# Gated linear attention and a rational gelu-like layer on one core: a new order of all steps and loads

## The chip, the cores and the metric

The kernel runs on one core of one Trainium2 chip. The metric is the time of one execution on the device in microseconds (us), as the median over runs. Engines are named as in the profile: PE is TensorE's matmul, PEld its weight load, DVE is VectorE, ACT is ScalarE, POOL is GpSimd, SP is SyncE.

## The reference

Two layers follow each other. The first is a linear attention with a gate per channel, for 4 batches and 8 heads, 768 tokens, 48 channels per head; the second works on its result as 3072 tokens by 384.

```python
f = 1 / (1 + exp(-f_logit))
for t in range(768):                                   # state: [B, H, 48, 48], from zero
    state = f[:, :, t, :, None] * state + einsum('bhd,bhe->bhde', k[:, :, t], v[:, :, t])
    y[:, :, t] = einsum('bhd,bhde->bhe', q[:, :, t], state)

x = y.transpose(0, 2, 1, 3).reshape(3072, 384)
h = x @ w_in                                           # 384 -> 2048
P = a[0] + a[1] * h + a[2] * h**2 + a[3] * h**3
Q = 1 + abs(b[0]) * abs(h) + abs(b[1]) * h**2
out = (P / (Q + 1e-6)) @ w_out                         # 2048 -> 384
```

## The kernel before

**Units.** The work is cut into 12 units of 256 tokens. Unit n is batch n % 4 and chunk n // 4, so four units in a row don't depend on each other, and unit n needs the state that unit n - 4 left. Each unit passes through all steps.

**The order is written out by hand.** A text named `ORDER` lists all steps, separated by semicolons, and the kernel's last loop calls the function of each in turn. Every engine and queue gets its instructions in that order and works them off in that order; between engines only the data dependences hold (semaphores are set by them). So a step that waits holds back everything behind it on its own engine or queue and nothing else. `sc 5 1 @1` means step sc of unit 5 with argument 1 in PSUM slot 1 (there are four, `@0` to `@3`). Arguments such as `8 16` are blocks of 128 of the 2048 columns of h, so `0 16` is a whole step and `8 16` a half; for f, k, q and the steps on them `2 4` is the second half of the heads.

**Attention steps.** `ld n f`, `ld n k`, `ld n q` load 384 KB each from SP's queue, `ld n v` loads from POOL's queue and converts to bf16. `ef`, `ls` (ACT) give log(1 + exp(-f)); `cs` (PE) sums it along the tokens; `A` and `ae` (ACT) are exponentials of that; `xa n 1` and `xa n 0` (DVE, or POOL where a `p` ends the step) multiply k and q by them; `T` (PE) transposes and `Te` (DVE, or ACT with `s`) copies the result from PSUM; `sc` (PE) gives scores, `mk` (DVE) masks them; `vm` (POOL) copies pieces of v; `yi` and `yb` (PE) make y; `ic`, `si` (PE) and `st` (DVE) carry the state on; `ye` (ACT with `s`, DVE with `v`) copies y to x.

**Layer steps.** `h` (PE) multiplies x by w_in, four blocks at a time; `hy` (ACT) copies it to SBUF. `sq` and `ab` (DVE) make h squared and its absolute value, scaled so that Q needs only their sum. That sum is made in one of three ways, half by half: `zv` adds on DVE, `zd` issues from POOL a DMA that accumulates in SBUF, `u` (PE) adds by two matmuls with the identity into PSUM. `lz` (or `ln`, after `u`) takes the logarithm and `ex` the exponential with scale -1, both on ACT: 1 / Q. For P, `p1` (DVE) makes a3 h + a2, `pm` multiplies by h squared, `p2` makes a1 h + a0, and the two are added by `tv` on DVE or by `ta`, again an accumulating DMA from POOL. `gm` (DVE) multiplies P by 1 / Q; `o` (PE) multiplies by w_out; `oe` copies the result from PSUM and `so` stores it from SP's queue, in two DMAs.

```python
def zv(n, m0, m1):
    return nc.vector.tensor_add(fl(big(s, "z"), m0, m1), fl(big(s, "z"), m0, m1), fl(big(s, "h2"), m0, m1))
def zd(n, m0, m1):
    return nc.gpsimd.dma_start(out=fl(big(s, "z"), m0, m1), in_=fl(big(s, "h2"), m0, m1), accum_op=ALU.add)
```

**Buffers.** f, k, q and v have three buffers each, hy and g three, the squares and z two. `ld 7 k` thus waits until `xa 4 1` has read its buffer, and `so` holds back the loads behind it on SP until `oe` is done. **Weights.** `wi 0 8`, `wi 8 16` (three DMAs each) bring w_in, four `wo` bring w_out, all converted to bf16, from POOL's queue. Constants come from `cz`, `cu`, `ci`, `cm`; `ab_`, `fa`, `fb`, `fr` load and prepare the coefficients.

Lines in the profile: L206 load, L214 w_in, L221 w_out, L284 `ef`, L317 `xa`, L360 `mk`, L457 `h`, L469 `hy`, L473 `sq`, L477 `ab`, L485 `u`, L495 `zv`, L499 `zd`, L503 `lz`, L508 `ex`, L513 `p1`, L518 `p2`, L523 `pm`, L527 `ta`, L531 `tv`, L535 `gm`, L544 `o`, L550 `oe`, L559 `so`.

Of the kernel before, what the change touches and what calls it, by code (L numbers as in the profile page):

```python
# [29 lines left out]
h 1 12 16 @2; hy 1 4 8; p1 0 0 16; ls 3; h 1 0 4 @3; lz 0 0 8; ab 0 8 16; cs 2 @1; pm 0 0 16; h 1 8 12 @0  # L30
hy 1 12 16; A 2 1; u 0 12 16 @2; p2 0 0 16; hy 1 0 4; xa 2 1; ae 2; A 2 0; u 0 8 12 @3; ln 0 12 16; tv 0 0 8
hy 1 8 12; xa 2 0; ef 4; ab 1 8 16; T 2 @1; ln 0 8 12; ab 1 0 8; cs 3 @2; sq 1 0 16; Te 2 s; si 2 0 @0; A 3 1
sc 2 0 @3; tv 0 8 16; sc 2 1 @1; ic 2; zd 1 0 8; A 3 0; ae 3; mk 2 0; ex 0 0 16; xa 3 1 0 4 p; u 1 8 12 @2
st 2 0; yb 2 0 2 @3; mk 2 1; vm 3 1; yi 2 1; si 2 1; xa 3 0; u 1 12 16 @1; ls 4; st 2 1; ld 6 q; yb 2 2 4
gm 0 0 8; ld 5 f; ln 1 12 16; cs 4 @0; ld 4 k; ln 1 8 12; gm 0 8 16; ld 6 f; T 3 @1; ld 6 k; ae 4; ye 2 s
p1 1 0 16; o 0 1 8 12 @2; ex 1 8 16; si 3 0 @3; o 0 0 8 12; pm 1 0 16; o 0 1 12 16; o 0 1 4 8; lz 1 0 8
o 0 0 12 16; o 0 0 4 8; p2 1 0 16; ef 5; o 0 1 0 4; Te 3; o 0 0 0 4; A 4 0; ta 1 8 16; A 4 1; ic 3; tv 1 0 8
sc 3 1 @1; ls 5; h 2 12 16 @0; oe 0 0 2 s; mk 3 1; xa 4 1 0 4 p; ld 8 f; ld 7 f; ef 6; sc 3 0 @2; ld 5 q; st 3 0
h 2 8 12 @1; ex 1 0 8; so 0 0 2; mk 3 0; vm 3 0; vm 4 1; si 3 1; xa 4 0; h 2 4 8 @2; hy 2 12 16; gm 1 8 16
# [10 lines left out]
hy 4 0 4; xa 7 0; ic 6 @3; hy 4 8 12; sc 5 0 @1; vm 5 1; ta 3 8 16; o 2 0 8 12 @2; mk 5 0; ef 9; o 2 0 12 16  # L50
vm 6 0; lz 3 8 16; vm 6 1; si 6 0; sq 4 0 16; o 2 1 4 8; yb 5 2 4 @0; yb 5 0 2; lz 3 0 8; yi 5 1; yi 5 0
ab 4 0 16; o 2 0 0 4; T 6 @1; ye 5 s; p1 4 0 16; zd 4 8 16; ls 8; o 2 0 4 8; ld 7 v; st 6 0; h 5 12 16 @0
ex 3 0 16; Te 6; zd 4 0 8; o 2 1 12 16; p2 4 0 16; si 6 1; o 2 1 0 4; h 5 0 4 @1; pm 4 0 16; hy 5 12 16
o 2 1 8 12; hy 5 0 4; h 5 8 12 @0; gm 3 0 8; oe 2 0 2 s; ta 4 8 16; h 5 4 8 @1; gm 3 8 16; hy 5 8 12; lz 4 8 16
# [557 lines left out]
```

## Time and profile before

| | |
|---|---|
| Time, median of 3 runs | 245.29 us (244.83 to 245.74) |
| The profiled execution: its own time, its span | 245.4 us, 243.7 us |
| Granted clock of TensorE, mean | 0.972 |
| Busy: PE, DVE, ACT, POOL | 201.7, 204.6, 196.2, 93.7 us |
| DMA packets of POOL's queue (q0) and of SP's (q1) | 24.92 MB and 18.88 MB |

The profile is of one execution. Busy time is the time in which an engine works on an instruction; DMAs are shown by their queue, packet by packet. "Idle before" tells which event ended an engine's wait. The 1.7 us between the profiled execution's time and its span lie before the first and after the last instruction of the program.

### The profile page before, as it was taken

What the parts mean: (1) busy time and instruction counts of PE and PEld (TensorE: products, weight loads), DVE (VectorE), ACT (ScalarE), POOL (GpSimd) and SP (SyncE); (2) the same over time, 40 slices, a digit from 0 to 9 for tenths busy, and PEclk for the clock granted to TensorE, in tenths of its full rate; (3) what the DMA queues carried; (4) which work ended last, traced back from release to release, by engine and by line L of the source; (5) the groups of instructions that cost most, each with busy time, mean ns of one, the idle gap of its engine ahead of it and who ended that gap; (6) DMA issues with size and microseconds to landing.
All of it is one profiled execution on the core that took longest, in us unless ns stands there. A gap on an engine that the chain in (4) does not pass through costs nothing.

```text
span 243.7 us, 7028 instructions
## 1 busy us (share of the span) xinstructions
PE 201.7 (83%) x3116; PEld 143.9 (59%) x3120; DVE 204.6 (84%) x194; ACT 196.2 (81%) x188; POOL 93.7 (38%) x105
## 2 busy tenths in 40 slices
PE   0468599669999969989829899999999799998792
PEld 0346378436677647767616757787676576854361
DVE  3266299999989999999665799999999999995950
ACT  3354059999999997979609999999999799968950
POOL 6084034040415495374053633654545323441000
PEclk9999889988999999999997999999999999999799
DMA  7999999998999985999959799999999858999352
GB/s 133 228 206 159 122 204 205 198 208 191 223 248 250 180 167 58 192 223 213 202 125 159 121 253 215 206 156 227 211 248 210 168 118 161 185 203 205 86 127 66
DMA packets 64382, 44.24 MB, mean 182 GB/s; under 512 B 53728, under 2 KB 58848, under 8 KB 64352
## 3 DMA queue, kind: packets, MB, share of 16 engines
q0 software_dynamic: 23088, 24.92, 62.8%
q1 hardware_dynamic: 40976, 18.88, 35.3%
q8 instruction: 24, 0.39, 0.7%
q10 hardware_dynamic: 288, 0.00, 0.1%
q14 instruction: 6, 0.05, 0.1%
HBM read 25.17 MB, written 4.72 MB: 123 GB/s over the span
## 4 chain that ended last, share of the span: by engine, by line
DMA 28%; DVE 18%; issue 18%; ACT 17%; PE 7%; POOL 6%; SPq 3%; POOLq 0%; ACTq 0%; DVEq 0%
DMA f<-in_f_logit_dram 9%; DMA g<-hy 6%; DMA w_in_sb<-in_moe_w_in_dram 5%; PE op L544 5%; DVE g L535 5%; ACT qi L508 4%; ACT hy L469 4%; ACT lq L503 4%; DMA v<-in_v_dram 4%; DMA z<-h 4%; SPq L206 3%; DVE h L473 3%; DVE g L513 2%; DVE hy L518 2%; DVE z L477 2%
## 5 line engine op out<-in xcount | busy, mean ns | idle before, releaser
L544 PE MATMUL op<-w_out_sb,g 128*128 128x384 bf16 x384 | 72.8, 337 | 4.1 <-DVE g L535 4.1
L457 PE MATMUL hp<-x,w_in_sb 128*128 128x256 bf16 x576 | 69.6, 275 | 6.2 <-DMA w_in_sb<-in_moe_w_in_dram 2.8
L457 PEld LDWEIGHTS <-w_in_sb 128*128 128x128 bf16 x576 | 56.2, 98 | 17.4 <-issue 5.6
L544 PEld LDWEIGHTS <-g 128*128 128x128 bf16 x384 | 36.9, 101 | 31.0 <-issue 5.5
L469 ACT CAST hy<-hp 128x1024 bf16<-128x1024 f32 x48 | 47.0, 1052 | 9.5 <-PE hp L457 9.5
L508 ACT ACTIVATE qi<-lq 128x2048 bf16<-128x2048 f32 (+1 forms) x19 | 45.1, 2374 | 2.3 <-DVE g L535 2.2
L503 ACT ACTIVATE lq<-z 128x2048 f32<-128x2048 bf16 x21 | 40.5, 1928 | 5.5 <-DMA z<-h 5.5
L499 POOL DMA_DIRECT2D z<-h x19 | 20.4, 1191 | 47.1 <-DVE z L477 31.9
L535 DVE TENSOR_TENSOR g<-g,qi 128x2048 bf16<-128x2048 bf16 (+1 forms) x19 | 30.5, 1627 | 6.9 <-ACT qi L508 5.9
L360 DVE TENSOR_TENSOR scm<-sc,mask 128x1024 bf16<-128x1024 f32 x24 | 28.7, 1215 | 7.5 <-PE sc L352 7.3
L527 POOL DMA_DIRECT2D g<-hy x18 | 19.1, 1109 | 38.2 <-DVE hy L518 17.5
L317 POOL TENSOR_TENSOR qkp<-k,A 128x768 bf16<-128x768 f32 x10 | 24.8, 2479 | 18.2 <-DMA k<-in_k_dram 9.1
L473 DVE TENSOR_TENSOR h<-hy 128x2048 bf16<-128x2048 bf16 (+1 forms) x16 | 28.0, 1751 | 0.2 <-ACT hy L469 0.2
L523 DVE TENSOR_TENSOR g<-g,h 128x4096 bf16<-128x4096 bf16 (+1 forms) x15 | 27.8, 1856 | 0.1
L284 ACT ACTIVATE f<-f 128x768 f32<-128x768 f32 (+1 forms) x13 | 10.8, 833 | 13.6 <-DMA f<-in_f_logit_dram 13.6
L331 PE MATMUL tp<-ident,qkp 128*128 128x128 bf16 x192 | 15.0, 237 | 7.9 <-POOL qkp L317 4.3
L312 ACT ACTIVATE A<-cs 128x768 f32<-128x768 f32 (+1 forms) x26 | 19.8, 800 | 0.7 <-PE cs L304 0.6
L367 POOL COPY vmp<-v 128x128 bf16<-128x128 bf16 x24 | 15.7, 802 | 10.8 <-DMA v<-in_v_dram 8.7
L206 POOL DMA_DIRECT2D v<-in_v_dram x12 | 14.1, 1179 | 12.1 <-PE y L373 11.3
L331 PEld LDWEIGHTS <-qkp 128*128 128x128 bf16 x192 | 12.9, 106 | 9.9 <-POOL qkp L317 4.7
L299 PE MATMUL cs<-lsp,Ui 128*128 128x384 bf16 (+1 forms) x39 | 11.1, 343 | 9.1 <-ACT lsp L289 8.8
L513 DVE TENSOR_SCALAR g<-hy,a_sb 128x4096 bf16<-128x4096 bf16 x12 | 17.7, 1471 | 1.0 <-ACT hy L469 1.0
...
## 6 DMA issues: line engine op xcount, KB each, us to landing
...
```

The lines of the kernel that those rows point to most:

```text
L317: i = (nc.gpsimd if eng == "p" else nc.vector).tensor_mul(s["qk"][:, x, :, hh, 0:D], s["qk"[x]][:, hh].rearrange("p h i d -> p i h d"), s[ ...
L331: nc.tensor.transpose(t[:, x, i, p, :], s["qk"][:, x, i, 2 * p:2 * p + 2, :].rearrange("t h d -> t (h d)"), ident)
L360: return nc.vector.tensor_mul(t, s["sc", g].rearrange("s r a i t -> s (r a) (i t)"), mb)
L457: nc.tensor.matmul(t[:, m - m0, :].rearrange("f (j t) -> f j t", j=UB), w_in_sb[:, kk, m * P:(m + 1) * P], s["x"][:, :, kk, :], start=(kk ...
L469: nc.scalar.copy(fl(big(s, "hy"), m0, m1), fl(s["hp", m0], 0, m1 - m0))
L473: return nc.vector.tensor_mul(fl(big(s, "h2"), m0, m1), fl(big(s, "hy"), m0, m1), fl(big(s, "hy"), m0, m1))
L503: nc.scalar.activation(fl(lq, m0, m1), fl(big(s, "z"), m0, m1), AF.Ln, scale=regs[2], bias=1.0 + 1e-6)
L508: nc.scalar.activation(fl(qi, m0, m1), fl(lq, m0, m1), AF.Exp, scale=-1.0)
L513: return nc.vector.tensor_scalar(fl(big(s, "g"), m0, m1), fl(big(s, "hy"), m0, m1), a_sb[:, 3:4], a_sb[:, 2:3], op0=ALU.mult, op1=ALU.add)
L523: return nc.vector.tensor_mul(fl(big(s, "g"), m0, m1), fl(big(s, "g"), m0, m1), fl(big(s, "h2"), m0, m1))
L535: return nc.vector.tensor_mul(fl(big(s, "g"), m0, m1), fl(big(s, "g"), m0, m1), fl(qi, m0, m1))
L544: nc.tensor.matmul(s["op", g][:, j, 0:DM], big(s, "g")[:, m, C * j:C * j + C], w_out_sb[:, m, :], start=(s["on", j] == 1), stop=(s["on", j ...
```

## The change

Only `ORDER` is replaced: 785 steps become 765. No function changes.

- Every step's place changes, the loads' and stores' on SP and POOL among them. On SP the sequence around unit 7 to 11 was `so 1, ld 8 q, ld 8 k, ld 7 k, ld 10 f, so 3, so 2, ld 9 q, ld 9 k, ld 11 f, ld 11 q, so 4, ld 10 k, ld 10 q, ld 11 k`; it becomes `ld 8 q, ld 7 k, ld 9 f, so 1, ld 8 k, so 2, ld 10 f, ld 11 f, ld 9 k, ld 9 q, ld 10 k, so 3, ld 10 q, so 4, ld 11 q, ld 11 k`.
- The 48 half sums (24 for Q, 24 for P): `zd` 19 to 16, `zv` 2 to 6, `u` 3 to 2 (six quarters to four), `ta` 18 to 19, `tv` 6 to 5. Accumulating DMAs go from 37 to 35, additions on DVE from 8 to 11.
- Halves become whole steps: `ex` 19 instructions to 14, `gm` 19 to 14, `sq` 16 to 13, `ab` 16 to 13, `pm` 15 to 13.
- `xa 1 1` goes from POOL to DVE (10 products on POOL become 9). `Te` on DVE: units 1, 4, 8, 10 and both halves of 0, instead of 1, 3, 6, 7, 10 and those halves; the others on ACT. `ye 6` goes from ACT to DVE. `oe` on DVE: units 7 and the second part of 11, instead of 4, 9 and that part.
- At the start, `cs 2`, `sc 1 0` and `sc 1 1` come ahead of `h 0 0 4`, and `wi 0 8` follows `vm 0 1`, no longer `ld 2 v`. The `wo` loads follow `ta 0 0 8`.

The diff, cut to the start, the places named here and the end:

```diff
@@ -17,80 +17,78 @@
 ORDER = """
-ld 0 k 2 4; cz 1; ld 1 v; ld 0 f 0 2; cz 2; cz 3; cz 0; ld 0 f 2 4; cu 0; ld 0 k 0 2; ld 0 v; ld 0 q 2 4
-ld 0 q 0 2; ci; ld 1 f; cu 1; ld 1 q; ef 0 0 2; ab_ b a; ab_ a a; cm; ld 1 k; ls 0 0 2; ef 0 2 4; cs 0 0 2 @0
-ld 2 f; ls 0 2 4; A 0 1 0 2; cs 0 2 4 @1; vm 1 1; A 0 1 2 4; A 0 0 2 4; xa 0 0 2 4; xa 0 1 2 4; xa 0 1 0 2
-T 0 2 4 @2; Te 0 2 4; ic 0 @3; ef 1; vm 0 1; ld 2 v; sc 0 1 @2; ae 0 2 4; ls 1; mk 0 1; wi 0 8; ae 0 0 2
-A 0 0 0 2; cs 1 @1; xa 0 0 0 2; fa; T 0 0 2 @2; ae 1; A 1 1; si 0 0; vm 0 0; wi 8 16; st 0 0; vm 1 0
-xa 1 1 0 4 p; Te 0 0 2; si 0 1; st 0 1; ef 2; sc 0 0 @0; yi 0 1 @2; mk 0 0; ls 2; ic 1 @3; fr; yb 0 2 4
-yb 0 0 2; A 1 0; si 1 0; ye 0 s; xa 1 0; vm 2 1; ld 4 q; T 1 @0; vm 2 0; ld 3 f; h 0 0 4 @1; ld 2 k; Te 1
-ld 3 k; ld 4 f; sc 1 0 @2; hy 0 0 4; ld 2 q; sc 1 1 @0; ld 3 q; mk 1 1; h 0 4 8 @1; mk 1 0; yb 1 2 4 @0
-hy 0 4 8; st 1 0; yb 1 0 2; fb; yi 1 1; sq 0 0 8; ld 4 v; h 0 12 16 @2; ye 1 s; wo 0 4; ab 0 0 8; h 0 8 12 @1
...
-A 5 1; ic 4 @3; ls 6; ab 2 8 16; yi 3 1; yb 3 2 4; ae 5; sq 2 0 8; ef 7; ld 9 f; zd 2 8 16; T 4 @0; ye 3 s
...
-ye 4 s; zd 3 0 8; oe 1 0 2 s; h 4 12 16 @3; gm 2 0 16; A 7 1; so 1 0 2; A 7 0; ld 8 q; h 4 4 8 @0; ld 8 k
-Te 5 s; pm 3 0 16; h 4 0 4 @2; ld 7 k; ld 10 f; hy 4 4 8; sc 5 1 @1; hy 4 12 16; h 4 8 12 @0; mk 5 1; ta 3 0 8
...
-st 6 1; xa 7 1 0 4 p; sc 6 0 @2; sc 6 1 @0; mk 6 0; o 3 0 4 8 @3; o 3 1 12 16; hy 5 4 8; vm 7 1; mk 6 1
-ta 4 0 8; cs 8 @2; ef 10; p1 5 0 16; yb 6 0 2 @1; A 8 0; yb 6 2 4; ex 4 8 16; yi 6 1; sq 5 0 16; yi 6 0
...
-u 11 12 16 @3; pm 11 0 16; o 9 1 8 12; o 9 1 0 4; o 9 0 4 8; o 9 0 0 4; ln 11 8 12; gm 10 8 16; o 9 0 12 16
-oe 8 0 2 s; gm 10 0 8; o 10 1 12 16 @2; ln 11 12 16; so 8 0 2; o 10 1 8 12; p2 11 0 16; o 10 0 0 4; ex 11 8 16
-o 10 0 8 12; tv 11 8 16; o 10 1 4 8; lz 11 0 8; o 10 1 0 4; gm 11 8 16; o 10 0 12 16; o 10 0 4 8; oe 9 0 2 v
-ex 11 0 8; o 11 1 8 12 @1; tv 11 0 8; so 9 0 2; o 11 0 8 12 @3; o 11 0 12 16; oe 10 0 2 s; gm 11 0 8
-o 11 1 12 16; so 10 0 2; o 11 0 0 4; o 11 0 4 8; o 11 1 4 8; oe 11 0 1 s; o 11 1 0 4; so 11 0 1; oe 11 1 2 v
-so 11 1 2
+ab_ b a; ld 0 f 0 2; cz 1; cu 0; ld 0 f 2 4; cz 3; cz 2; cz 0; ld 0 k 0 2; cu 1; ld 1 f; ld 0 q 2 4; ld 0 v; cm
+ld 0 q 0 2; fa; ci; ef 0 0 2; ld 0 k 2 4; ld 1 v; si 0 0 @0; ef 0 2 4; ld 2 f; ls 0 0 2; ls 0 2 4; cs 0 0 2 @1
+ab_ a a; ld 1 k; cs 0 2 4 @2; ef 1; A 0 0 0 2; A 0 1 0 2; A 0 1 2 4; ae 0 0 2; A 0 0 2 4; ls 1; xa 0 0 2 4
+ld 1 q; xa 0 0 0 2; ae 0 2 4; cs 1 @3; xa 0 1 2 4; xa 0 1 0 2; T 0 2 4 @1; ae 1; A 1 0; ld 2 q; vm 0 1; wi 0 8
+ic 0; A 1 1; Te 0 2 4; T 0 0 2 @2; ef 2; st 0 0; ld 3 f; si 0 1; ls 2; Te 0 0 2; sc 0 1 @1; wi 8 16; st 0 1
+ld 2 k; cs 2 @3; xa 1 1; xa 1 0; sc 0 0 @2; A 2 1; fb; vm 0 0; T 1 @0; A 2 0; mk 0 0; ae 2; fr; mk 0 1
+si 1 0 @3; ic 1; yi 0 1 @2; st 1 0; yb 0 2 4; Te 1; yb 0 0 2; ld 4 f; sc 1 0 @1; ye 0 s; ld 3 v; sc 1 1 @0
+mk 1 0; si 1 1; vm 1 1; vm 1 0; h 0 0 4 @2; mk 1 1; ld 2 v; st 1 1; xa 2 0; h 0 4 8 @1; hy 0 0 4; ld 4 q
+yi 1 1 @0; hy 0 4 8; yb 1 2 4; yb 1 0 2; ab 0 0 8; ef 3; h 0 12 16 @3; sq 0 0 8; ye 1 s; ld 3 q; ls 3
+h 0 8 12 @2; zv 0 0 8; hy 0 12 16; cs 3 @1; xa 2 1; hy 0 8 12; h 1 4 8 @0; lz 0 0 8; ld 6 f; sq 0 8 16
...
+ta 0 0 8; yb 2 0 2; cs 4 @0; wo 12 16; ab 1 0 16; T 3 @2; wo 0 4; ae 4; vm 3 0; st 3 0; ye 2 s; wo 8 12
+p1 1 0 16; si 3 1; A 4 1; h 2 0 4 @1; wo 4 8; Te 3 s; st 3 1; pm 1 0 16; h 2 4 8 @3; A 4 0; sc 3 0 @2; hy 2 4 8
...
+o 0 0 8 12 @3; sq 2 0 16; ln 1 8 12; si 4 0; h 3 4 8 @0; ls 6; lz 1 0 8; T 4 @2; p1 2 0 16; zd 2 0 8; o 0 1 0 4
...
+yi 4 1 @2; yi 4 0; gm 1 0 16; yb 4 0 2; oe 0 0 2 s; yb 4 2 4; so 0 0 2; cs 6 @0; ye 4 s; ld 6 q; h 4 4 8 @1
...
+ld 7 k; sc 5 0 @3; o 1 0 8 12; vm 5 0; st 5 1; xa 6 1 0 4 p; ld 9 f; mk 5 1; o 2 0 0 4 @1; lz 3 0 8; o 2 1 12 16
...
+T 6 @0; so 1 0 2; o 2 0 8 12; ld 8 k; ye 5 s; vm 6 0; st 6 0; zd 4 0 8; p2 4 0 16; ls 7; si 6 1; o 2 1 0 4
+Te 6 s; h 5 12 16 @3; st 6 1; zv 4 8 16; cs 7 @2; oe 2 0 2 s; pm 4 0 16; h 5 0 4 @0; A 7 0; so 2 0 2; ld 10 f
...
+sc 6 0 @1; hy 5 4 8; cs 8 @2; mk 6 1; xa 7 1 0 4 p; lz 4 8 16; o 3 0 12 16 @3; o 3 0 8 12; mk 6 0; ta 4 0 8
...
+pm 5 0 16; h 6 4 8 @0; o 3 0 0 4; o 3 1 0 4; ld 10 k; vm 7 0; st 7 1; hy 6 0 4; xa 8 0; h 6 12 16 @2; ef 10
...
+cs 9 @2; p2 5 0 16; ld 10 q; lz 5 8 16; o 4 1 8 12 @1; mk 7 0; o 4 0 8 12; ta 5 8 16; lz 5 0 8; ab 6 0 16
...
+p1 11 0 16; ln 11 0 4; so 8 0 2; o 9 1 12 16; ln 11 4 8; gm 10 0 8; o 9 0 8 12; ex 10 8 16; o 9 0 12 16
+pm 11 0 8; o 10 1 4 8 @2; o 9 0 4 8; p2 11 0 16; ex 11 0 8; o 10 0 4 8; o 9 1 4 8; gm 10 8 16; o 10 0 0 4
+oe 9 0 2 s; tv 11 0 8; lz 11 8 16; o 10 1 12 16; so 9 0 2; o 10 0 12 16; gm 11 0 8; o 10 1 8 12; ex 11 8 16
+o 10 1 0 4; pm 11 8 16; o 11 1 0 4 @3; o 11 0 0 4 @0; tv 11 8 16; o 11 1 4 8; o 10 0 8 12; gm 11 8 16
+o 11 0 4 8; oe 10 0 2 s; o 11 1 12 16; so 10 0 2; o 11 1 8 12; o 11 0 12 16; oe 11 1 2 v; o 11 0 8 12; so 11 1 2
+oe 11 0 1 s; so 11 0 1
 """
```

More of the change, by code (lines that the diff above doesn't have):

```diff
@@ L30 @@
[L30 to L39, printed above, removed]
@@ L50 @@
[L50 to L54, printed above, removed]
@@ new lines @@
+p1 7 0 16; o 5 0 0 4; hy 8 12 16; ic 9; ab 7 0 16; lz 6 0 8; sc 9 0 @3; sc 9 1 @0; o 5 0 4 8; tv 6 0 8
+o 5 1 8 12; zd 7 0 8; lz 6 8 16; o 5 1 4 8; mk 9 1; xa 10 1 0 4 p; mk 9 0; h 8 4 8 @0; ex 6 0 16; vm 9 1
+zd 7 8 16; xa 10 0; h 8 8 12 @3; vm 9 0; st 9 0; ld 11 v; p2 7 0 16; h 8 0 4 @2; pm 7 0 16; hy 8 8 12
+o 5 1 12 16; o 5 1 0 4; hy 8 4 8; o 5 0 8 12; hy 8 0 4; cs 11 @3; gm 6 0 16; ta 7 8 16; oe 5 0 2 s; ic 10 @0
+ta 7 0 8; A 11 0; yi 9 0 @2; yi 9 1; yb 9 2 4; A 11 1; sq 8 0 16; yb 9 0 2; ae 11; T 10 @1; ye 9 s; lz 7 0 8
```

80 lines of the change are left out of this document (41 added, 39 removed).

## The prediction

> **What bounds the kernel now.** I read the page first (shares and slices), then the sums by stretch, then the timelines of VectorE, ScalarE and SP around the one long gap, and last the DMA queues in short windows. From the page:
>
> ```profile
> span 243.7 us, 7028 instructions
> PE 201.7 (83%) x3116; PEld 143.9 (59%) x3120; DVE 204.6 (84%) x194; ACT 196.2 (81%) x188; POOL 93.7 (38%) x105
> ...
> PE   0468599669999969989829899999999799998792
> ...
> DVE  3266299999989999999665799999999999995950
> ```
>
> Three engines have almost equal work, and VectorE (DVE) has most. Its idle time is 243.7 - 204.6 = 39.1 us. The sums by stretch (length, then busy time by engine) tell where that lies:
>
> ```profile
> 0.00:40.00 40.00, 24.74 (x420) 19.00 (x421) 21.26 (x47) 17.73 (x27) 17.76 (x34) 0.96 1.18 178
> 40.00:120.00 80.00, 70.38 (x1153) 50.58 (x1154) 78.30 (x67) 75.17 (x75) 31.47 (x28) 0.98 1.05 196
> 120.00:140.00 20.00, 13.94 (x206) 10.06 (x206) 12.89 (x10) 13.35 (x13) 9.28 (x8) 0.91 0.80 141
> 140.00:220.00 80.00, 75.69 (x1252) 55.20 (x1252) 79.32 (x62) 74.93 (x67) 34.38 (x35) 1.00 1.01 197
> 220.00:243.70 23.70, 16.90 (x90) 9.07 (x89) 12.84 (x11) 15.06 (x10) 0.82 (x1) 0.93 0.54 119
> ```
>
> The third busy time is VectorE's: idle 18.7 us at the start, 1.7 in 40:120, 7.1 in 120:140, 0.7 in 140:220, 10.9 at the end. So outside start and end VectorE is the bound, with one hole. The timelines of ScalarE and of SP name its cause:
>
> ```profile
> 127.47 0.84 ACT L284 ACTIVATE f<-f 128x768 f32<-128x768 f32 x1 [6.65 <-DMA f<-in_f_logit_dram]
> ...
> 74.36 0.76 SPq L206 DMA_DIRECT2D f<-in_f_logit_dram  x1
> 95.90 1.26 SPq L559 DMA_DIRECT2D out_dram<-osb  x2
> 97.25 1.98 SPq L206 DMA_DIRECT2D q<-in_q_dram  x1
> 99.34 7.25 SPq L206 DMA_DIRECT2D k<-in_k_dram  x2
> 106.64 7.13 SPq L206 DMA_DIRECT2D f<-in_f_logit_dram  x1
> ```
>
> SP stood from 75 to 95.9 us behind the store of unit 1 (`so 1 0 2` waits for `oe 1`). Four loads were then issued together, `ld 7 k` and `ld 10 f` last, and f of unit 10 took 20.8 us to land (median of that load on the page: 6.8 us). Why so long, the DMA queues show in the window 108:112, while accumulating sums move:
>
> ```profile
> q0 software_dynamic: 204, 0.77, 96.6%
> q1 hardware_dynamic: 204, 0.08, 10.1%
> ```
>
> Both queues got 204 packets in 4 us: one each in turn. A sum's packet is 4096 bytes, a load's 384, so POOL's queue took 0.77 MB and SP's 0.08. A load of 384 KB (1024 packets) beside sums needs 1024 / 204 x 4 = 20 us, about what was seen; by q0's rate a sum of 512 KB takes 2.7 us.
>
> **The change, part by part.** The arithmetic of the reference is the same; ORDER is new. Prices are spacings of successive starts in the timeline.
>
> *VectorE's work.* Additions there go from 8 to 11 halves (`zv` 2 to 6, `tv` 6 to 5): 3 x 1.14 (50.83 to 51.97 in the timeline) = +3.4. Halves merged into whole steps: `sq` 3, `gm` net 5, `pm` net 2, each saving 2 x 1.14 - 2.20 = 0.08, and `ab` 3 x 0.08: -1.0. `xa 1 1` moves from POOL to VectorE: +0.9. `Te`: one of full size fewer: -1.1. `ye 6` comes, one `oe` goes: 0.9 - 0.9. Sum **+2.2 us** (1.5 to 3), all of it on the path, since VectorE is the bound.
>
> *POOL's products beside VectorE.* The groups of L513 and L518 last 1.47 and 1.53 us in the mean, 1.33 where undisturbed; one at 81.02 took 3.71 while POOL worked on `xa 5 1`. 24 x 0.17 = 4.1 us for 10 products; 9 remain: **-0.4** (all 4.1 gone, or 4 more).
>
> *The hole.* For each load I added the VectorE work listed between its issue and its first user, and the DMA time of the sums and v loads listed in between (2.7 and 2.3 us each). Before: `ld 7 k` has 15.5 us against 16.0 of DMA time, `ld 10 f` 17.8 against 18.7: just these two were late. After: 17.9 against 7.3 and 16.0 against 8.2. `ld 8 k`, behind `so 1`, has 16.3 against 8.2, `ld 9 f` 19.7 against 12.8. The thinnest of the later loads are `ld 10 q` (24.1 against 23.8) and `ld 11 q` (15.0 against 13.3). Stores still stand between loads on SP, but fewer loads that are soon needed stand behind one. I take 6 of the 7.1 us back, and leave 1.1 for a thin one: **-6.0** (-7.1 to 0).
>
> *Coarser steps.* A whole `gm` now waits for a whole `ex` (3.52 us on ScalarE) in units 1, 6 and 7; for 4, 7 and 8 the list leaves only 3.4 to 3.6 us of VectorE work between the two. Before, one such wait was 3.2 us long, 5.9 in all. **+1.0** (0 to 4).
>
> *The sums.* 35 instead of 37: 2 x 2.7 us less for the DMA engines, -8 matmuls for `u` on PE and two issues of about 1.1 us fewer on POOL. All beside VectorE: 0. If the cover goes (a `lz` that waits for its sum cost ScalarE 5.5 us in all), it is worth up to -2. The list leaves most sums of units 4 to 9 more room than before (`ta 4 0 8` 10.6 us against 8.0, `zd 6 0 8` 13.9 against 8.1).
>
> *w_out.* Its four loads move from behind `ld 4 v` of the start to behind `ta 0 0 8`. Before, the third landed 16.3 us after the first was issued (35.5 to 51.7), and the first `o` began at 59. Now `wo 8 12` is third, and its first user `o 0 0 8 12` stands 14.4 us of VectorE work behind the first issue: 2 us late, of which I take half, as PE then has h of unit 3 behind it but VectorE has a gelu in hand: **+1.0** (0 to 4).
>
> *ScalarE* gets one `Te` more (1.77) and merges (-0.4): +1.4, beside VectorE (9.9 us idle in 40:120 and 140:220 together): 0. If that idle time were gone, +1.4.
>
> *The start.* VectorE begins in earnest at 34.3 (first `sq`). The w_in loads come at 14.0 to 18.5, behind a v load, and gate h: the chain of waits has one of them landing at 28.16, and the upper half lets `h 0 12 16` go only after 33.8. Now `wi 0 8` waits for `vm 0 1`, thus for v of unit 0 alone, and `sc 1 0`, `sc 1 1` stand ahead of `h 0 0 4` on PE, so that masks and products run while w_in lands. VectorE work ahead of the first gelu step grows from 16.0 to 18.2 us: if gelu starts at the same time, **-2.2**. v 0, the first on its queue at about 3.3, with the 7.7 us of the first v load now lands near 11; that would issue w_in 3 us sooner, so -5; the other bound, +10, is the first rival.
>
> *The end.* From the last `gm` on, 16 matmuls and two stores follow, as before; ScalarE has 17.0 us listed behind the last `hy` instead of 16.2, VectorE 18.8 instead of 16.2, where it also waited for 2.6: **0** (-1 to +2).
>
> Sum: 2.2 - 0.4 - 6.0 + 1.0 + 1.0 - 2.2 = -4.4. The profiled execution took 245.4 us (span 243.7), the median of three is 245.3, so it stands for them: 245.4 - 4.4 = **241.0 us**.
>
> The Trainium skill's page "DMA: Bandwidth & Descriptors", section "Queues, rings and completion order", says that a DMA engine drains a whole packet, typically 9 to 17 descriptors, before it turns to the next queue. If a turn carried that many rows of a load, loads would hardly suffer beside sums or w_in, and the first rival would fall away. The 204 against 204 above, at 384 bytes a packet of SP's queue, speak against that.
>
> **Rivals.** *Loads starved by w_in at the start (slower).* In the new order SP still has k and q of unit 1 to bring (ninth and tenth load) when w_in begins. Both stand before `mk 0 0` on VectorE (`xa 1 1`, `xa 1 0`), thus before y, x and h of unit 0. Here 2.7 MB of SP's loads, as many as the new order has up to q of unit 1, landed by 17.9, and only then w_in moved alone. In 26:32, with both, the queues carried:
>
> ```profile
> q1 hardware_dynamic: 982, 0.37, 80.0%
> q0 software_dynamic: 333, 0.37, 49.3%
> ```
>
> That is one load in 6 us. If w_in issued at 11 moves from 13 on and needs the 15.8 us of here (18 to 33.8), it ends at 28.8 and q 1 lands near 30. `xa 1 0`, `fb`, both masks (3.8), then y, x, `sc 1`, two h and two `hy` (7 us by the timeline) bring the first gelu to 40.8: 6.5 later than 34.3, less the 2.2 of work done, +4.3 where the sum has -2.2: 247.5. With w_in slowed to 31.5 and q 1 at 34.3 it is 251.8. I take 249. It decides at one point: whether q 1 has landed when w_in's packets begin. For it speaks the alternation; against it, that `vm 0 1` and `wi 0 8` may come as late as before.
>
> *The hole moves (no change).* `so 2` has `ld 10 f`, `ld 11 f`, `ld 9 k`, `ld 9 q` and `ld 10 k` behind it. If `oe 2` is late by as much as `oe 1` was (SP's 22 us), one is again late: 5 of the 6 us come back, 246.0. Also if the new order does not keep loads and sums apart.
>
> *The start gains in full (faster).* w_in 3 us sooner, loads in time: -5 instead of -2.2, and neither +1.0: 241.0 - 2.8 - 2.0 = 236.2.
>
> **Chances.** Forecast 0.50 (its own range 238 to 244: the start by 2, the hole by 1, coarse steps and w_out by 1 each), full gain 0.13, moved hole 0.14, starved start 0.23. A measurement of this kernel tells about 0.5% (1.2 us) from no change, so faster is below 244.1: 0.63, same 0.14, slower, above 246.5: 0.23. The range, 236.0 to 249.0, takes in the forecast, the full gain, the moved hole and the nearer half of the starved start; some 0.06 is left below it and 0.11 above.
>
> **What would show it.** Right: no wait of `ef` or of POOL's product for a load above 2 us between 60 and 220, VectorE busy near 207, idle there under 5 us, the first `ab` of unit 0 by 35 us. Wrong at the start: `xa 1 0` waiting for q beyond 25 us. Wrong in the middle: `gm` waiting for `qi`, or SP behind a store for over 15 us with an `ef` late after it.

## The result, and the profile after

The new order took 235.21 us (median of 4 runs, 232.19 to 236.92), the old one beside it 245.51 (244.83 to 247.11): a ratio of 0.9496 [0.9383, 0.961]. The change makes the kernel faster, as forecast, but by more than twice the 4.4 us that were forecast: the median lies 5.8 us below the forecast of 241.0 and 0.8 below the lower end of its range. Two further measurements gave 233.94 against 245.80, 0.9544 [0.9489, 0.9599], and 233.45 against 246.53, 0.9537 [0.9435, 0.9639]. (Ratios leave out disturbed executions, so they need not equal the quotient of the medians.)

The profiled execution took 232.19 us and is the lowest of its four. Its page answers to the one of before:

```profile
span 230.5 us, 6995 instructions
PE 196.3 (85%) x3112; PEld 141.8 (61%) x3112; DVE 204.2 (89%) x184; ACT 195.8 (85%) x183; POOL 84.8 (37%) x102
...
PE   0493599867999999899999988999996998899992
...
DVE  5251788999999999999999999999999999989860
```

VectorE is busy for as long as before (204.6 us then); the span is shorter because it waits less: 26.3 us instead of 39.1. The dent in its slices past the middle is gone. The sums by stretch (length, then PE, PEld, VectorE, ScalarE, POOL; clock, DMA share, GB/s) show where:

```profile
0.00:40.00 40.00, 24.38 (x427) 18.37 (x428) 22.70 (x49) 18.71 (x30) 10.98 (x26) 1.00 1.18 195
40.00:120.00 80.00, 73.64 (x1308) 54.05 (x1307) 80.00 (x64) 80.00 (x76) 38.41 (x40) 1.00 1.11 212
120.00:140.00 20.00, 18.02 (x294) 12.86 (x292) 20.00 (x16) 20.00 (x18) 13.92 (x11) 1.00 1.05 204
140.00:210.00 70.00, 64.62 (x999) 47.83 (x997) 68.88 (x47) 64.05 (x52) 21.19 (x27) 1.00 0.94 174
210.00:230.50 20.50, 15.68 (x93) 8.64 (x90) 12.60 (x11) 13.05 (x11) 0.25 (x1) 0.98 0.45 104
```

From 40 to 140 VectorE has no idle time at all, and ScalarE none either. The waits of VectorE between the start and the end, before (the four longest) and after (all), in the view that adds up waits (us in total, times, longest):

```profile
DVE g L535 <- ACT qi L508: 3.2, 1, 3.2
DVE T L338 <- PE tp L331: 3.0, 1, 3.0
DVE scm L360 <- PE sc L352: 1.1, 2, 0.8
DVE g L513 <- ACT hy L469: 1.0, 1, 1.0
```

```profile
DVE z L475 <- ACT hy L467: 1.1, 1, 1.1
DVE h L471 <- ACT hy L467: 1.1, 1, 1.1
```

Both waits after lie at the edges (35.4 and 205.4 us). Two loads were late before, k of unit 7 and f of unit 10. On SP k of unit 7 is now issued ahead of the store of unit 1, together with f of unit 9:

```profile
93.79 1.69 SPq L204 DMA_DIRECT2D k<-in_k_dram  x1
95.53 1.61 SPq L204 DMA_DIRECT2D f<-in_f_logit_dram  x1
99.43 4.22 SPq L557 DMA_DIRECT2D out_dram<-osb  x2
103.75 0.89 SPq L204 DMA_DIRECT2D k<-in_k_dram  x1
```

Both landed 11 us after their issue; `ld 7 k` took 22.8 us before. `ld 10 f`, which took 20.8 us, still stands behind a store (`so 2`, issued at 109.2) and landed in 7.3 us. No engine waits for a load between 40 and 210. At the start VectorE still waits, for k and q of unit 1, while w_in moves:

```profile
20.38 0.96 DVE L315 TENSOR_TENSOR qkp<-k,A 128x768 bf16<-128x768 f32 x1 [4.03 <-DMA k<-in_k_dram]
24.35 0.96 DVE L315 TENSOR_TENSOR qkp<-q,A 128x768 bf16<-128x768 f32 x1 [3.02 <-DMA q<-in_q_dram]
...
35.38 0.69 DVE L475 TENSOR_SCALAR z<-hy 128x2048 uint16<-128x2048 uint16 x1 [1.13 <-ACT hy L467]
```

Three VectorE operations before and two after took 1.5 to 2.5 us longer than the shortest of their form, and each stands beside a product of POOL. One pair before, and then one after:

```profile
81.02 3.71 DVE L518 TENSOR_SCALAR hy<-hy,a_sb 128x4096 bf16<-128x4096 bf16 x1
```

```profile
81.53 2.10 POOL L317 TENSOR_TENSOR qkp<-k,A 128x768 bf16<-128x768 f32 x1
```

```profile
170.25 4.17 DVE L521 TENSOR_TENSOR g<-g,h 128x4096 bf16<-128x4096 bf16 x1
```

```profile
170.12 2.14 POOL L315 TENSOR_TENSOR qkp<-k,A 128x768 bf16<-128x768 f32 x1
```

For all comparisons below I split a profile in four, from VectorE's timeline: its busy time, and its idle time before the first `ab`, from there to the last `hy`, and after that. "Stretch" is the part of the busy time by which operations exceed the shortest of their form; busy time less stretch is called work below.

| profile | span | busy | of it stretch | idle: start | middle | end |
|---|---|---|---|---|---|---|
| old order | 243.7 | 204.6 | 7.9 | 18.5 | 9.7 | 10.9 |
| new order | 230.5 | 204.2 | 6.0 | 17.2 | 1.1 | 7.9 |
| new order, again | 232.3 | 204.3 | 5.9 | 18.8 | 1.5 | 7.7 |
| e1: two loads ahead | 233.9 | 204.2 | 7.8 | 16.6 | 3.3 | 9.9 |
| e16: and the end in halves | 234.9 | 204.5 | 8.0 | 19.0 | 3.0 | 8.3 |
| a6: new, two loads behind | 234.9 | 205.5 | 7.2 | 17.8 | 3.9 | 7.7 |
| a2: new, 38 sums | 233.2 | 199.6 | 4.1 | 19.0 | 7.0 | 7.6 |
| a5: new, unit 0 first, mended | 228.8 | 204.0 | 6.6 | 15.8 | 1.5 | 7.6 |
| a8: and two products moved | 228.8 | 202.2 | 2.7 | 16.8 | 2.1 | 7.6 |

The old start, unchanged in the old order, e1 and e16, has 16.6 to 19.0 us of idle time: one profile can't tell 2 us there. About 1.1 us of the old order's 10.9 at the end belong to that profile too: see "The end" below.

### The profile page after: what moved, and what is told of

Its sections match the earlier page's. It is cut to its first block, busy times and chain, and to the rows that moved or that the text cites. A ratio compares the mean times of both kernels' runs of the same rounds, so it can differ in the third digit from the quotient of the medians.

```text
span 230.5 us, 6995 instructions
## 1 busy us (share of the span) xinstructions
PE 196.3 (85%) x3112; PEld 141.8 (61%) x3112; DVE 204.2 (89%) x184; ACT 195.8 (85%) x183; POOL 84.8 (37%) x102
## 4 chain that ended last, share of the span: by engine, by line
DVE 45%; ACT 19%; DMA 14%; issue 11%; PE 6%; SPq 3%; DVEq 0%; ACTq 0%; POOLq 0%
DVE g L533 7%; DMA q<-in_q_dram 7%; DVE h L471 6%; DVE scm L358 6%; ACT lq L501 6%; DVE g L521 5%; ACT qi L506 4%; DMA z<-h 4%; PE hp L455 4%; DVE g L511 4%; DVE hy L516 4%; ACT hy L467 3%; SPq L204 3%; DVE z L475 3%; DMA g<-hy 3%
## 5 line engine op out<-in xcount | busy, mean ns | idle before, releaser
L542 PE MATMUL op<-w_out_sb,g 128*128 128x384 bf16 x384 | 69.2, 326 | 1.3 <-issue 0.7
L467 ACT CAST hy<-hp 128x1024 bf16<-128x1024 f32 x48 | 49.2, 1073 | 4.1 <-PE hp L455 4.1
L501 ACT ACTIVATE lq<-z 128x2048 f32<-128x2048 bf16 x22 | 43.0, 1983 | 2.7 <-DMA z<-h 2.7
L506 ACT ACTIVATE qi<-lq 128x4096 bf16<-128x4096 f32 (+1 forms) x14 | 44.5, 3187 | 0.1
L497 POOL DMA_DIRECT2D z<-h x16 | 15.4, 967 | 41.2 <-DVE z L475 11.8
L471 DVE TENSOR_TENSOR h<-hy 128x4096 bf16<-128x4096 bf16 (+1 forms) x13 | 27.5, 2116 | 1.1 <-ACT hy L467 1.1
L533 DVE TENSOR_TENSOR g<-g,qi 128x4096 bf16<-128x4096 bf16 (+1 forms) x14 | 27.7, 1978 | 0.9 <-ACT qi L506 0.8
L315 POOL TENSOR_TENSOR qkp<-k,A 128x768 bf16<-128x768 f32 x9 | 18.4, 2049 | 6.6 <-ACT A L310 6.6
L315 DVE TENSOR_TENSOR qkp<-q,A 128x768 bf16<-128x768 f32 (+1 forms) x13 | 11.6, 898 | 6.8 <-ACT A L310 3.8
L516 DVE TENSOR_SCALAR hy<-hy,a_sb 128x4096 bf16<-128x4096 bf16 x12 | 16.8, 1402 | 0.0
```

The source lines that it names most:

```text
L315: i = (nc.gpsimd if eng == "p" else nc.vector).tensor_mul(s["qk"][:, x, :, hh, 0:D], s["qk"[x]][:, hh].rearrange("p h i d -> p i h d"), s[ ...
L467: nc.scalar.copy(fl(big(s, "hy"), m0, m1), fl(s["hp", m0], 0, m1 - m0))
L471: return nc.vector.tensor_mul(fl(big(s, "h2"), m0, m1), fl(big(s, "hy"), m0, m1), fl(big(s, "hy"), m0, m1))
L501: nc.scalar.activation(fl(lq, m0, m1), fl(big(s, "z"), m0, m1), AF.Ln, scale=regs[2], bias=1.0 + 1e-6)
L506: nc.scalar.activation(fl(qi, m0, m1), fl(lq, m0, m1), AF.Exp, scale=-1.0)
L533: return nc.vector.tensor_mul(fl(big(s, "g"), m0, m1), fl(big(s, "g"), m0, m1), fl(qi, m0, m1))
```

## Experiments

Theory A of the first four: the loads held behind one store made the hole, and that hole is the largest part of the gain. Rivals: the accumulating sums beside the loads made it, wherever the loads stand; or the gain comes from the new start.

**Two loads ahead of the store.** The old order with one edit.

```diff
-xa 5 1 0 4 p; ls 7; o 1 1 0 4
+xa 5 1 0 4 p; ls 7; ld 7 k; ld 10 f; o 1 1 0 4
-h 4 0 4 @2; ld 7 k; ld 10 f; hy 4 4 8
+h 4 0 4 @2; hy 4 4 8
```

> The order of before, with two loads moved on SP and nothing else: k of unit 7 and f of unit 10 now stand ahead of the store of unit 1, behind ls 7. Theory A (the hole in 120:140 came from these two loads, held behind a store and then starved by sums): they land before 100 us, ScalarE's wait of 6.7 us for f 10 and POOL's of 9.1 us for k 7 go, VectorE's idle time in 100:140 falls from 8.1 us to under 2, and the time from 245.4 to 238.5 to 240. Theory B (the loads were only the last link, the middle is tight everywhere and another wait takes their place): 243 to 246, with a new wait of 4 us or more between 100 and 150.

237.75 us against 243.49, 0.9794 [0.9711, 0.9877]. The middle's idle time fell from 9.7 to 3.3. In the stretch in which VectorE and ScalarE had 12.89 and 13.35 us of work before:

```profile
120.00:140.00 20.00, 18.96 (x327) 14.07 (x325) 20.00 (x18) 20.00 (x18) 9.14 (x10) 1.00 0.97 199
```

By the ratio, two moved loads out of 785 steps are worth 2.1% (5.0 us), somewhat under half of the change's 4.6 to 5.0%.

**Four sums on VectorE instead.** The old order; SP as it was. `tv` and `zv` take the place of accumulating DMAs that moved while the late loads did.

```diff
-ta 3 0 8   -ta 3 8 16   -zd 4 8 16   -zd 4 0 8
+tv 3 0 8   +tv 3 8 16   +zv 4 8 16   +zv 4 0 8
```

> The order of before and its loads, with four sums between 95 and 125 us (both halves of P of unit 3, both of Q of unit 4) made by VectorE's addition instead of an accumulating DMA: SP's queue is as it was, but POOL's queue has 11 us less to move beside the late loads. VectorE gets 4 x 1.14 = 4.6 us more. Theory A (sums starve the loads): k 7 and f 10 land in 4 to 10 us instead of 22.8 and 20.8, the hole of 7.1 us shrinks to under 1, and the time is 245.4 + 4.6 - 6.5 = 243.5. Theory B (SP's queue is slow by itself at four loads in a row): they land as late as before, the hole stays, and the time is 249 to 250.

243.42 us, 0.9968 [0.986, 1.0076]. The middle's idle time fell to 3.0 although SP issued k of unit 7 at 103.4 and f of unit 10 at 106.7, as late as before (101.5 and 106.6); they landed in 8.7 and 6.7 us; VectorE's busy time grew by 3.6. So the hole needed both: loads issued late, and sums that fill the DMA engines while they move. Either cure removes it, and only the first is free.

**New start, old rest; old start, new rest.** The hybrids cut the two lists at `ls 3` and at `ye 1 s`.

> The new order up to ls 3 (units 0 and 1 up to x, unit 2 up to its first product), then the old order for all that is left. Theory A (the new start is worth what VectorE's idle time in 0:40 says, 18.7 to 17.3 us, and the hole of the middle belongs to the old rest): 243.5 to 245, with the hole in place. Theory B (the start is worth more than the first 40 us show, since loads that come earlier help later): 238 to 241.

247.78 us, 1.0144 [0.9996, 1.0293]: the hole is there (4.7 us at 129.6, and 2.6 more at 173), and the start alone gains nothing.

> The old order up to ye 1, then the new order for all that is left. Theory A (the gain lies in the middle and at the end): 235 to 238, VectorE idle under 2 us between 45 and 200 us. Theory B (the new middle holds only together with the new start): above 240, with waits for loads or sums between 40 and 100 us.

241.66 us, 0.996 [0.9866, 1.0055]: theory B's number, with a wait for a load between 40 and 100 as it named it. But VectorE's timeline shows that this is a wait at the seam, which neither full order has, since the old start loads q of unit 2 late:

```profile
45.93 0.96 DVE L315 TENSOR_TENSOR qkp<-q,A 128x768 bf16<-128x768 f32 x1 [7.60 <-DMA q<-in_q_dram]
```

So I mended it:

```diff
-ld 3 v; si 1 1; st 1 1; xa 2 0; ab 0 0 8; ef 3
+ld 3 v; si 1 1; st 1 1; ab 0 0 8; ef 3
-ab 0 8 16; A 3 0
+ab 0 8 16; xa 2 0; A 3 0
```

> The hybrid of the old start and the new rest again, with its one seam wait taken away: xa 2 0, which stood on VectorE for 7.6 us until q of unit 2 landed, now follows ab 0 8 16. Theory A (the gain of the change lies almost wholly behind the start: no hole, no waits for a whole ex, an end 3 us shorter): the earlier hybrid's 241.7 less most of 7.6, so 233.5 to 236.5, within 1.5 us of the new order; VectorE's idle time between the first gelu step and the last hy falls from 10.5 to below 4. Theory B (the new start is worth some us by itself, or the wait merely moves to the next step): 238.5 or more.

236.13 us (234.97 to 239.69; before 245.81), 0.9717 [0.9406, 1.0028]. The median lies in theory A's range, 1 to 3 us above the new order's medians on other chips, but the interval is too wide to settle it: that nearly all of the gain lies behind the start is not shown by this run.

**The new order with the two loads put back.** `ld 7 k` and `ld 9 f` go behind the second store.

```diff
-sc 5 1 @2; ld 7 k; sc 5 0 @3
-xa 6 1 0 4 p; ld 9 f; mk 5 1
-so 2 0 2; ld 10 f
+so 2 0 2; ld 7 k; ld 9 f; ld 10 f
```

> The new order with one thing put back as in the old one: ld 7 k and ld 9 f stand behind the store so 2 0 2 on SP, together with ld 10 f. Theory A (where two loads stand about a store is what made the hole): k of unit 7 is issued near 109 instead of 93.8, POOL's product xa 7 1 or a later ef waits for its load, the middle's idle time on VectorE rises from 1.1 to 4 to 7, and the time is 3 to 6 us above the new order's. Theory B (the hole came from the accumulating sums beside the loads, and in the new order loads land in 7 to 12 us wherever they are issued): within 1 us of the new order.

234.68 us, 0.9673 [0.9503, 0.9843]: 1 us above the new order by the medians of other chips, some 3 us by the ratios, with an interval too wide to tell. The middle's idle time is 3.9 instead of 1.1 to 1.9, but only 0.9 of it lies near the moved loads (at 121); the rest comes behind 187. So the hole did not come back. k of unit 7 was issued at 109.64, 8 us later than in the old order, but landed in 5.1 us. The timeline of POOL and the packets of 110:116 tell why:

```profile
114.86 1.80 POOL L315 TENSOR_TENSOR qkp<-k,A 128x768 bf16<-128x768 f32 x1 [8.51 <-DMA k<-in_k_dram]
```

```profile
q1 hardware_dynamic: 3105, 1.45, 91.7%
q0 software_dynamic: 21, 0.04, 3.6%
```

POOL itself waited for this load and issued no sum meanwhile, so SP's loads had the DMA engines almost to themselves. In the old order five sums were issued between 101.3 and 114.5, ahead of the product that waited. What made the hole was the pair, late loads with sums listed ahead of their user, not the place about the store alone.

**Sums back on DMAs.** The new order with 38 accumulating sums, each of the three new ones beside its unit's other `zd`.

```diff
-zv 3 0 8   -zv 4 8 16   -zv 5 8 16
+zd 3 0 8   +zd 4 8 16   +zd 5 8 16
```

> The new order with three of its additions on VectorE (half of Q of units 3, 4 and 5) made again by accumulating DMAs: 38 of these, 8 additions. Theory A (VectorE is the bound and sums are hidden): VectorE's busy time 3.4 us less, time 3 us less, 0.5 to 1 of it lost to waits. Theory B (POOL's queue is full there, so the sums come late or starve the loads): ScalarE waits for z, or for f 9 or f 10, or POOL for k 7 or k 8, by 3 us or more in all between 80 and 130 us, and the time is the same or longer.

238.43 us, 0.9698 [0.963, 0.9766], against 0.9544 for the new order beside it (below): slower by 3.8 us by the ratios, and the two intervals do not meet. Against the repeat of the new order VectorE is busy for 4.7 us less (1.8 of it stretch) and has 5.5 us more idle time in the middle. The waits of ScalarE and VectorE there:

```profile
ACT lq L501 <- DMA z<-h: 4.9, 3, 2.8
```

```profile
DVE scm L358 <- PE sc L350: 3.5, 4, 2.1
```

The longest of VectorE's waits can be followed: ScalarE stood 1.73 us for a sum at 99.6, its `ex` and `ye` came late, PE waited 1.70 us for x, and VectorE 2.14 us at 114.9 for scores. The other waits are 0.2 to 0.7 us each, and their causes stay open; of ScalarE's 4.9 us the new order has 2.9 too. The three additions that I booked as +3.4 us of pure cost save more than they cost.

> The new order as it is, once more, so that the three variants of it below have their reference on the same chip. Expected: 0.945 to 0.960 of before; by the phases of VectorE's idle time as in its profile: some 17 us before the first gelu step, under 2 us from there to the last hy, some 8 us after it.

The order itself, again: 233.94 us, as given above.

**Halves again.** The new order with `ab` (3), `sq` (3), `pm` (3), `gm` (5) and `ex` (6) cut in halves once more, half behind half in place, for example

```diff
-gm 1 0 16
+gm 1 8 16; gm 1 0 8
```

> The new order with the merged steps cut into halves again where before had them (ex of units 1, 4, 6 to 9, gm of 0, 1, 3, 6, 7, some sq, ab and pm). VectorE has 13 instructions more: 13 x 0.08 = 1.0 us, ScalarE 6 x 0.08 = 0.5. Theory A (whole steps only save these gaps; the wait of a whole gm for a whole ex that I had priced at +1.0 does not occur): +1 us. Theory B (whole steps cost a wait somewhere): the same or up to 1 us less.

234.82 us, 0.9582 [0.9523, 0.9641]; +0.9, as theory A has it, but within the scatter. VectorE's busy time grew by 0.7, and its waits are as they were. So whole steps cost nothing here; that they gain the 1 us which the merging should save is not clear of the scatter.

**The end.** The old order with the two loads ahead and, at the end, `ex 10` in halves, with `gm` and the `o` steps of unit 10 in the order of the halves (the diff is cut to the main steps).

```diff
-lz 10 0 8
+lz 10 0 8; ex 10 0 8
-p1 11 0 16
+p1 11 0 16; ex 10 8 16
-zd 11 0 8; ex 10 0 16
-gm 10 8 16 ... gm 10 0 8; o 10 1 12 16
+gm 10 0 8 ... gm 10 8 16; o 10 1 4 8
```

> The old order with two edits: ld 7 k and ld 10 f ahead of the store (as in the first experiment, there 0.979 of the old order), and at the end the whole ex 10 cut into two halves, each right behind its lz, with gm 10 0 8 ahead of gm 10 8 16 and the o steps of unit 10 in that order. Theory A (in the old end VectorE waited 2.6 us for the whole ex 10 and later steps followed from that): the stretch behind the last hy shrinks from 27.5 to 25 to 26 us, VectorE's idle time in it from 9.9 to about 8, and the time is 1.5 to 2.5 us below the first experiment's, near 0.970 of the old order. Theory B (PE's o steps and the stores set the end whatever VectorE does): less than 0.7 us, 0.977 to 0.982.

235.63 us (233.96 to 237.68), 0.9736 [0.9605, 0.9868], on a chip where the old order took 245.81. The interval holds both theories' ratios; the profile speaks for A: from the first experiment's to this one, the time from the last `hy` to the end shrank from 27.5 to 25.9 us. The wait for the whole `ex` in the old order, which is gone here (a wait of 1.1 us for a sum of P is left):

```profile
225.59 2.36 DVE L535 TENSOR_TENSOR g<-g,qi 128x2048 bf16<-128x2048 bf16 x2 [2.56 <-ACT qi L508]
```

That left open whether these two edits are all of the gain. Beside the new order:

> The new order itself once more, on the same chip as the next three, so that their times can be set against it. Both theories: within 1.5 us of 234.5.

> The old order with the two edits (two loads ahead of the store, the whole ex 10 near the end in halves) once more, beside the new order on one chip. Theory A (these two edits hold nearly all of the change's gain, and the other 700 moved steps cancel out): within 1 us of the new order. Theory B (the rest of the new order, its fewer small waits and fewer stretched VectorE operations, is worth something by itself): 1.5 to 3 us above the new order.

233.45 us for the new order, 236.61 for the two edits, 0.9698 [0.9619, 0.9777], with the old order at 246.53. By the ratios the two edits hold 3.0 of 4.6%, some 7 of 11 us, and the rest of the new order is worth 3.9 us (3.2 by the medians): theory B. By the two profiles (234.9 against 232.3) it lies in the stretching (8.0 against 6.3), the middle (3.0 against 1.9), the end (8.3 against 7.6) and the start (19.0 against 18.5), less 1.5 us of work that the new order has more.

**The start.** Unit 0's masks, y, x and two of its h ahead of unit 1's products (the diff is cut to its first part).

```diff
-st 0 1; ld 2 k; cs 2 @3; xa 1 1; xa 1 0; sc 0 0 @2
+st 0 1; mk 0 1; ld 2 k; cs 2 @3; sc 0 0 @2; fb; vm 0 0; mk 0 0; fr; yi 0 1 @0; yb 0 2 4; yb 0 0 2; ye 0 s
+xa 1 1; A 2 1; xa 1 0; h 0 0 4 @1; ld 4 f; ld 3 v; h 0 4 8 @0; hy 0 0 4; A 2 0; ae 2; hy 0 4 8; T 1 @2; ab 0 0 8
```

> The new order with its start rewritten: unit 0's masks, y and x come ahead of unit 1's products (xa 1 1, xa 1 0, A 2 0) and h 0 0 4 and h 0 4 8 ahead of T 1, so that nothing of unit 0 waits for the k and q of unit 1, which land at 20.3 and 24.3 us because w_in is moving. Theory A (the starved loads hold up the start, the named first rival at a smaller price): first gelu step at 27 to 29 us instead of 35.4, VectorE's idle time before 40 us falls from 17.3 to 13 or 14, time 3 to 4 us below the new order. Theory B (the start is set by the upper half of w_in, landing at 30.9, whatever is done before): gain under 1 us.

234.01 us, 0.9553 [0.9494, 0.9611], as the new order. The first `ab` comes at 28.5 instead of 36.9, but 3.0 us of it go back at 37.5, in a wait for the upper half of h. With the other two h and their `hy` ahead as well:

> The new order, with all of unit 0's way to its gelu layer (masks, y, x, all four h with their hy) ahead of unit 1's products, so that the first gelu step does not wait for k and q of unit 1. Theory A (the order at the start matters once the third and fourth quarter of h come early too): the last hy of unit 0 moves from about 39.4 to about 36, and the time is 2 to 3 us below the new order's. Theory B (the start is bound by the arrival of w_in's upper half and by f of unit 3, so what is gained before is waited for later, as when only the first two quarters came early): within 0.8 us of the new order.

234.14 us, 0.9684 [0.955, 0.9819]: by the profile (15.8 us idle at the start, 4.8 in the middle) the gain is given back again, now in another wait. PE stood 3.0 us for `ls 3`, which was listed on ScalarE behind `lz 0 0 8` and `ye 1`, and VectorE got it as a wait for the state:

```profile
47.62 0.56 DVE L445 TENSOR_TENSOR state<-sv,ae 128x384 bf16<-128x384 f32 x1 [2.47 <-PE sv L416]
```

Two steps of ScalarE turned about:

```diff
-ef 3; hy 0 8 12
+ef 3; ls 3; hy 0 8 12
-lz 0 0 8; ye 1 s; ld 3 q; ls 3; sq 0 8 16
+ye 1 s; lz 0 0 8; ld 3 q; sq 0 8 16
```

> The new order with all of unit 0 first, as before, and two ScalarE steps turned about: ls 3 right behind ef 3, and ye 1 ahead of lz 0 0 8. In the earlier version the gelu work began 8 us sooner (28.5), but PE stood 3.0 us for ls 3 before h of unit 1, and VectorE got 2.5 us of it as a wait for st 2 0 at 45. Theory A (that wait was all that took the gain back): it falls below 0.7 us and the time is 1.5 to 2.5 us below the new order beside it, a version that beats both. Theory B (it is always given back, since k and q of unit 2 and 3 and w_in arrive when they arrive): within 0.8 us.

230.37 us (228.62 to 231.77), 0.9409 [0.9326, 0.9493], against 233.45 for the new order on the same chip. The same row has no wait now:

```profile
45.06 0.56 DVE L446 TENSOR_TENSOR state<-sv,ae 128x384 bf16<-128x384 f32 x1
```

The start was worth 3 us after all, but the change didn't have them.

**Products of POOL.** First all nine on VectorE (`xa n 1 0 4 p` becomes `xa n 1`, units 3 to 11):

> The new order with the nine products that POOL makes (xa n 1 of units 3 to 11) made by VectorE in the same places of the order; POOL then issues DMAs and copies v only. By itself that is 9 x 0.87 = 7.8 us more on VectorE. What is read is the sum of the time that VectorE operations took beyond the shortest of their form (6.0 us in the new order, 7.9 in the old). Theory A (the operations of 3 to 4 us are VectorE beside a product of POOL): no operation is stretched by over 1 us, the sum falls to 1 to 2.5, VectorE's busy time grows by 3 to 5 us, and the time by 3 to 7. Theory B (the stretching has another cause, such as DMAs): two or three operations still take 3 us or more, the sum stays at 5 to 6, and busy grows by 7 to 8.

237.73 us, 0.9702 [0.9603, 0.9802], 4.3 above the new order beside it. The sum of stretching fell to 3.0, no operation is longer than the shortest of its form by more than 0.40 us, and VectorE's busy time grew by 3.8 instead of 7.8. Then only the two products beside which an operation was stretched, in the best version so far, with that version beside it:

```diff
-xa 9 1 0 4 p   -xa 11 1 0 4 p
+xa 9 1         +xa 11 1
```

> The version with all of unit 0 first and the two ScalarE steps turned about, once more, beside the next one. Both theories: 229.5 to 231.5, at 0.937 to 0.945 of the old order.

> That version with the products xa 9 1 and xa 11 1 made by VectorE, because they are the two beside which a VectorE operation was stretched there: L511 at 133.9 took 3.10 us instead of 1.33, L521 at 168.5 took 4.17 instead of 2.27, 3.7 us in all. Theory A (the product is the cause and nothing else takes its place): VectorE's busy time changes by 2 x 0.87 - 3.7 = -1.9 and the time by -1 to -2. Theory B (other products then fall beside such an operation, or VectorE waits for the k or exponential that POOL used to wait for): -0.5 to +1.

230.22 us (229.40 to 230.59), 0.9474 [0.94, 0.9549]; the version beside it 232.13 (229.69 to 235.28; 229.5 to 231.5 was expected), 0.9529 [0.9396, 0.9663]; the old order 244.23. The squaring product that took 4.17 us is back at its length:

```profile
169.26 2.28 DVE L521 TENSOR_TENSOR g<-g,h 128x4096 bf16<-128x4096 bf16 x1
```

Busy time went from 203.8 to 202.2, stretching from 6.1 to 2.7. That is theory A for the cause. For the time it is not settled: the intervals overlap, and the spans are alike (229.1 and 228.8), since start and middle have 1.3 us more of idle time in this profile. Its median is the lowest here, but by the ratios the version without this edit did better on another chip (0.9409), so which of the two is faster stays open.

## Why the prediction was right and wrong

The mechanism of the largest term, the hole, was right. What failed is the sum around it: every entry missed, all but the start's in the same direction, and the largest miss is the end. The profile's change of -13.2 us against the -4.4 of the sum, by its own terms:

| step | forecast | measured |
|---|---|---|
| VectorE's work | +2.2 | +1.5 |
| POOL's products beside VectorE | -0.4 | -1.9 |
| the hole | -6.0 | -7.1 |
| coarser steps | +1.0 | 0 |
| w_out | +1.0 | 0 |
| waits of the middle outside the hole | not in the sum | -1.5 |
| the start | -2.2 | -1.3 |
| the end, up to the last `gm` | 0 | -1.8 |
| behind the last `gm` | 0 | -1.1 |

Work is busy time without stretching (196.7 to 198.2). The profile is of a low execution; the repeat, with a start of 18.8, has -11.4.

- **The hole: right.** Place, cause and cure were as argued; moving the two loads took 6.4 us of idle time away. The count of DMA time between a load's issue and its user held for every later load too: `ld 10 q` and `ld 11 q`, which I called thin, made nobody wait. The 1.1 us kept for a thin one was not needed.
- **The end: the step that failed.** I set "listed work behind the last `hy`" of ScalarE and VectorE side by side, found a little more of it, and booked 0. But before, neither engine was the bound there: the two halves of `lz 10` waited 0.70 and 2.15 us for their sums, and VectorE 2.56 us for the whole `ex 10` behind them. The second of these waits and the `ex`, before, and the longest wait for an `ex` at the end, after:

```profile
220.00 1.91 ACT L503 ACTIVATE lq<-z 128x2048 f32<-128x2048 bf16 x1 [2.15 <-DMA z<-h]
221.94 3.62 ACT L508 ACTIVATE qi<-lq 128x4096 bf16<-128x4096 f32 x1
```

```profile
215.60 1.23 DVE L533 TENSOR_TENSOR g<-g,qi 128x2048 bf16<-128x2048 bf16 x1 [0.66 <-ACT qi L506]
```

The wait of 2.6 was in my text, and I did not ask what would become of it. From the last `hy` to the last `gm`, VectorE's idle time fell from 2.9 to 1.1 us; halving that one `ex` in the old order brought it from 3.0 to 1.4. The other 1.1 us, behind the last `gm`, are not a gain of the new order. PE had 25 matmuls of `o` left there before, and after it had the 16 that I had counted. But with the old end unchanged it also had 16 in e1 and with four sums on VectorE, and there the kernel ended 7.4 us after the last `gm` as in the new order, not 8.5. TensorE's granted clock was 0.83 in 225:235 of the old order's profile and 1.00 in the same part of those two; with the new start and the old rest it was 0.83 again, and 25 matmuls were left. So this 1.1 us goes with the clock of a profile and is luck in the comparison.
- **Coarser steps, w_out: booked, and not there.** No `gm` waits for `qi` in 40:210. I took "only 3.4 to 3.6 us of VectorE work between the two" for too little against an `ex` of 3.52 us, but that was about enough, and halving the steps again took no wait away.
- **POOL's products: right row, wrong size.** I took the mean over 24 operations and counted products, 10 against 9. What matters is which two or three products begin beside an operation that reads and writes SBUF: three before (6.4 us), two after (3.65 us). Beside the other seven VectorE mostly read PSUM (`mk`, `st`, `Te`) or ended what it had begun, and lost nothing. The Trainium skill's page "SBUF — State Buffer", section "SBUF: two separate sides", says that GpSimd and certain VectorE operations, those with two SBUF inputs among them, share a port pair under an exclusive lock: the one that starts first has it for its whole instruction, and the other is blocked. The trace agrees for the pair at 170: the operation took 1.90 us more, the product 2.14, of which 2.01 lay behind the operation's start. It does not agree on the order everywhere: at 81.02 and 186.73 before and at 135.63 after, the product began 0.51, 0.14 and 0.19 us behind the operation, and it was still the operation that grew (by 2.4, 2.5 and 1.8 us).
- **The start: no gain to speak of.** Over the profiles with this start (17.2 to 19.1) and with the old one (16.6 to 19.5, with four sums on VectorE the longest) its idle time is the same within 1 us in the mean. The -2.2 stood under "if gelu starts at the same time", and it starts 1.1 us later, in the repeats 2.3 to 2.6. My rival's mechanism did happen: w_in, issued 5 us sooner (8.96), moves while k and q of unit 1 do, which land at 20.29 and 24.33 and cost 7 us of waiting. What I priced wrongly is its consequence: w_in landed 3 to 5 us sooner as well, so the first gelu step came 1 to 3 us later and not 6.5. The condition "q beyond 25 us" was missed by 0.65.
- **The signs named:** VectorE's idle time in 60:220 and the waits for loads are as foretold. Its busy time is 204.2 and not near 207, from the stretching and a smaller work term; the first `ab` came at 35.4, not by 35.
- **The hole moves:** it did not, though `ld 10 f` stands behind `so 2`.
- **The range** reached 236.0 below because the one faster rival put only the start's further gain and the two dropped costs of +1.0 on top of the forecast. The other gains that came, stretching within its bound of -4.1 and the end beyond its bound of -1, were never added to these.

The rule on packets that the prediction weighed (the Trainium skill's page "DMA: Bandwidth & Descriptors", section "Queues, rings and completion order": 9 to 17 descriptors before a turn) still has the trace against it where POOL's queue is full of sums, if a packet of the profile is what the page calls a descriptor. My count of 204 against 204 was not enough for that, since equal long turns would give it as well; the times of the packets are. In 109:112 of the old order 117 of 137 packets of sums, and in 120:122 91 of 93, start within the last 6 ns of a load's packet (some 30 and 16 would by chance): a sum's turn was one packet and, as the counts are equal, a load's turn too. In the new order's window 94:104 the count looks like the rule:

```profile
q1 hardware_dynamic: 3703, 1.40, 58.9%
q0 software_dynamic: 288, 1.05, 53.5%
```

That is 13 to 1. It is no turn of 13, though: POOL's queue was busy for only half of the time, and SP's packets ran in the gaps. By 2 us pieces, 94:96 had 1482 of SP's packets and none of POOL's, and 100:102, with POOL's queue at 88.0%, had 328 against 89, while before, in 120:122, with POOL's queue at 96.8%, it was 113 against 117.
